# Two PSUM banks in turn for the products with v and three instead of four for scores and maxima, from the MLP's third chunk on

## The chip, the cores and the metric

The kernel runs on one core of one Trainium2 chip. Its time is device microseconds of one execution: the median of 3 runs of the kernel before is 1242.78 us (1240.4 to 1245.14). The core's engines work in parallel, each through its own instructions in order: PE (TensorE, with its weight loads shown apart as PEld), DVE (VectorE), ACT (ScalarE), POOL (GpSimd) and SP, which here issues DMAs. They wait for each other through semaphores.

Matmul results go to PSUM, which this kernel uses as eight banks, 0 to 7, each a tile of 128 x 512 fp32 numbers that holds one matmul's result or one running sum at a time. Before PE may write a bank anew, the engine that reads the old content must be done with it.

## The reference

64 heads (8 batches of 8), 576 positions, head size 64; then an MLP over 4608 tokens, 512 to 2048 to 512. All in fp32.

```python
log_f = np.log(np.clip(f, 0.0001, 1.0))
cum = np.cumsum(log_f, axis=-1)
scores = (q @ k.T) / sqrt(64) + cum[:, None] - cum[None, :]
scores = where(causal, -1e9, scores)
scores = scores - max(scores)                 # over a row
attn = exp(scores); attn = attn / (sum(attn) + 1e-9)
x = attn @ v                                  # heads side by side: 4608 x 512
h = maximum(x @ w_in, 0)
out = (h * h) @ w_out
```

## The kernel before, in words

**Attention.** A head is cut into six units (`UNITS`), each a piece of the transposed scores: one block of up to 128 keys against a stretch of 64 to 448 queries. The loop at its end goes through *slots*, one unit of one head each, six slots to a head. In a slot:

- the unit's **score** (L352 and L355 for the heads from the fifteenth on, L346 before): one bank of the turn `s`. ScalarE reads it with Exp into `p` (L365), GpSimd masks the diagonal (L367), and at the next slot's start the result is split in two parts for fp32 accuracy: `ph` by ScalarE (L380), `pl` by VectorE (L381).
- the **product with v** of the unit two slots back (L390, L391, L392: the parts pl and ph against the parts of v). The late queries of a head (256 to 575) are summed over five units in one bank of the turn `av`; the early ones (0 to 255) are done in the head's last such slot in another tile of that turn. When a sum is complete, ScalarE copies it out, the values by L426 and the denominators by L427. A head's first product (unit 0, late queries, 128x320) comes one slot after the early queries of the head before.
- of the head after it, the row **maxima**, six to a head in slots 1 to 4, here called m0 to m5 (L313: 256, 320, 448, 320, 192 and 64 columns). VectorE masks and reduces each in its bank (L319, two instructions: the reduction and the reading of its accumulator). Once the MLP runs, the maxima have no banks of their own; they draw from the turn `s`, as the scores do (`m=[]`, so that `bank` takes `banks["s"]`).

**MLP.** The tokens go in 18 chunks of 256, and a chunk in 16 steps. A step has two halves: `mlp1` (L478, 12 matmuls of 256 columns into the bank `h`; then Relu r and its square gh by ScalarE, L486 and L488; r times r, g, and its remainder gl by VectorE, L487 and L489) and, for the step before, `mlp2` (L501, 6 matmuls of 512 columns into the banks `o0` and `o1`, which hold a chunk's output through its 16 steps). `fill` spreads these halves over the slots, so that PE has them between the attention's short matmuls. When a new chunk's x is due, VectorE splits it (L465, L466).

**Order.** The order on PE, ScalarE, VectorE and GpSimd is the order in which the program is written (`in_order`). So an instruction that waits holds up everything behind it on its engine.

**Banks.** `bank(use)` takes the first number of a use's list and puts it at the end. The uses' lists change as the program goes on: with the first chunk of the MLP, the second and the third (`mlp_half`). The third chunk begins while the eighteenth head is under way, and its lists stay to the end. From then on: bank 4 for h, 6 and 7 for the outputs, and 0, 1, 2, 3, 5 for attention.

Of the kernel before, what the change touches and what calls it, by code (L numbers as in the profile page):

```python
# [33 lines left out]
def decay_attention_relu2_kernel(  # L34
# [45 lines left out]
    banks = {"av": [0, 6], "s": [1, 2, 3], "m": [4, 5], "h": [4], "o0": [6], "o1": [7]}  # L80
# [373 lines left out]
    def split_x(c, finished):  # L454

        if c >= NCHUNK:
            return
        if ("x", c) not in mst:
            mst["x", c] = [wk.tile([P, NCC, T], F32R, name=x, bufs=1) for x in xnames[c % 2]], c * T
        (xh, xl), t0 = mst["x", c]  # L460
        while t0 < (c + 1) * T and t0 // S < finished:
            b = t0 // S
            t1 = min((b + 1) * S, (c + 1) * T)
            o, i = slice(t0 - c * T, t1 - c * T), slice(t0 - b * S, t1 - b * S)
            nc.vector.tensor_copy(out=xh[:, :, o], in_=xts[b][:, :, i])  # L465
            nc.vector.tensor_tensor(  # L466
                out=xl[:, :, o], in0=xts[b][:, :, i], in1=xh[:, :, o].bitcast(F32), op=ALU.subtract,
            )
            t0 = t1
        mst["x", c] = (xh, xl), t0  # L470

    def mlp1(c, fc):
        xh, xl = mst["x", c][0]
        ph = bank("h")
        w = split_w[2 * fc].rearrange("p s (c f) -> p s c f", f=P)
        for k, (s, x) in enumerate(((1, xh), (0, xh), (0, xl))):
            for cc in range(NCC):
                nc.tensor.matmul(  # L478
                    ph[:, :T], w[:, s, cc], x[:, cc, :],
                    start=(cc == 0 and k == 0), stop=(cc == NCC - 1 and k == 2),  # L480
                )
        r = wk.tile([P, T], F32, name="r", bufs=1)
        g = wk.tile([P, T], F32, name="g", bufs=1)
        gh = wk.tile([P, T], F32R, name="gh")
        gl = wk.tile([P, T], F32R, name="gl")
        nc.scalar.activation(out=r, in_=ph[:, :T], func=AF.Relu)  # L486
        nc.vector.tensor_tensor(out=g, in0=r, in1=r, op=ALU.mult)  # L487
        nc.scalar.activation(out=gh, in_=r, func=AF.Square)  # L488
        nc.vector.tensor_tensor(out=gl, in0=g, in1=gh.bitcast(F32), op=ALU.subtract)  # L489
        mst["g", c, fc] = (gh, gl)  # L490

    def mlp2(c, fc):
        if fc == 0:
            mst["o", c] = [bank(f"o{t}") for t in range(NTT)]
        gh, gl = mst.pop(("g", c, fc))
        w = split_w[2 * fc + 1]
        for t in range(NTT):
            po = mst["o", c][t]
            ts = slice(t * P, (t + 1) * P)
            for k, (g, s) in enumerate(((gh, 1), (gl, 0), (gh, 0))):  # L500
                nc.tensor.matmul(  # L501
                    po, g[:, ts], w[:, s],
                    start=(fc == 0 and k == 0), stop=(fc == NF - 1 and k == 2),
                )
            if fc == NF - 1:
                osb = wk.tile([P, DM], F32, name="osb")
                nc.scalar.copy(out=osb, in_=po)
                nc.sync.dma_start(out=out[c * T + t * P:c * T + (t + 1) * P, :], in_=osb)
# [5 lines left out]
    def next_step():  # L514

        for c in range(NCHUNK):
            fc = ahead[c]
            if fc < NF and len(split_w) >= 2 * (fc + 1):
                return c, fc
            if fc < NF and c > 0:  # L520
                return None

    def mlp_half(finished):
        if halves[0] % 2:
            if len(steps) > 1:
                mlp2(*steps[-2])
        else:
            step = next_step()
            if step is None:
                return False  # L530
            c, fc = step
            if fc == 0:
                if c == 0:
                    banks.update(s=[1, 2, 3, 5], m=[], av=[0])
                if c == 1:
                    banks.update(s=[1, 2], o0=[3], o1=[5])
                if c == 2:
                    banks.update(s=[1, 2, 3, 5], o0=[6], o1=[7])
                split_x(c, finished)
            if fc > 0 and ("x", c + 1) not in mst and (c != 1 or ahead[0] == NF):  # L540
                split_x(c + 1, finished)
            mlp1(c, fc)
            ahead[c] += 1
            steps.append(step)
        halves[0] += 1
        return True
# [35 lines left out]
    def fill(n, part):  # L582

        b = sum(r <= n for r in ready)
        if b == 0:
            return
        r0 = ready[b - 1]
        r1 = ready[b] if b < B else r0 + H * NU
        limit, before = (2 * NF * (x * S // T) for x in (b, b - 1))
        goal = before + (limit - before) * (n - r0 + part) / (r1 - r0)  # L590
        if b == 1 and len(split_w) == NW:

            if not pace:
                pace.append((n + part, halves[0]))
            n0, h0 = pace[0]
            goal = h0 + (limit - h0) * (n + part - n0) / (r1 - n0)
        while halves[0] < min(goal, limit):
            split_last()
            if not mlp_half(b):
                break  # L600
# [71 lines left out]
    while halves[0] < 2 * NCHUNK * NF:  # L672
        mlp_half(B)
# [41 lines left out]
```

## Time and profile before

| | |
|---|---|
| median of 3 runs | 1242.78 us |
| the profiled execution | 1241.21 us |
| its span, first to last instruction | 1239.5 us |
| PE busy | 1179.0 us, 95% |
| PEld (weight loads, beside PE) | 1047.0 us, 84% |
| VectorE busy | 785.6 us, 63% |
| ScalarE busy | 701.3 us, 57% |
| GpSimd busy | 383.4 us, 31% |
| granted TensorE clock, mean | 0.992 |

PE is the engine with the least room. It is busy 95% of the span, and after the first fifth nearly all of the time; the attention of the first heads, with the weights' preparation beside it, fills that first fifth. From about 1090 us on only the MLP is left.

The trace gives each instruction's start and duration. For matmuls the end is modelled, so that consecutive ones overlap on paper: a matmul of 320 columns is shown as some 0.31 us long while the next starts 0.15 us after it. PE can thus wait without an idle gap being shown, and the distance from one start to the next tells more than the gaps.

### The profile page before, as it was taken

To read this page: it belongs to the slowest core of one execution; us is meant where nothing else is said; L and a number is where in the kernel's file an instruction comes from. 1 tells how busy PE (TensorE), PEld (TensorE's weight loads), DVE (VectorE), ACT (ScalarE), POOL (GpSimd) and SP (SyncE) were. 2 spreads that over 40 slices of the span, in tenths; PEclk is the share of its full clock that TensorE was granted. 3 is DMA by queue.
4 is the path that set the end of the run, shared out by engine and by line. 5 is a ranking of instruction groups with operands and counts; after the bars stand their busy time and mean duration, and the time that the engine had idled before them with its cause. 6 is when DMAs were issued, how large, how long until landed. Compare 5 with 4: busy or idle time off the path is not lost.

```text
span 1239.5 us, 23297 instructions
## 1 busy us (share of the span) xinstructions
PE 1179.0 (95%) x7652; PEld 1047.0 (84%) x7652; DVE 785.6 (63%) x2042; ACT 701.3 (57%) x1720; POOL 383.4 (31%) x576
## 2 busy tenths in 40 slices
PE   3777899999999999999999999999999999999998
PEld 2555677888999899999899989998999899999997
DVE  7658777667676767666656666677676767533332
ACT  3555455566666666665565666666666666632332
POOL 4333223333333433333222233334333333200000
PEclk9998899999999999999999999999999999999999
DMA  8867631112121212121202121211121212000000
GB/s 198 181 145 182 165 100 27 51 33 58 41 58 33 51 32 58 41 58 26 58 17 53 32 58 36 54 36 49 41 58 41 58 41 58 12 27 1 18 18 17
DMA packets 115640, 71.91 MB, mean 58 GB/s; under 512 B 97384, under 2 KB 97384, under 8 KB 115520
## 3 DMA queue, kind: packets, MB, share of 16 engines
q1 hardware_dynamic: 114400, 66.30, 21.9%
q0 software_dynamic: 1120, 4.13, 1.6%
q8 instruction: 61, 1.00, 0.3%
q14 instruction: 59, 0.48, 0.1%
HBM read 60.20 MB, written 9.88 MB: 57 GB/s over the span
## 4 chain that ended last, share of the span: by engine, by line
PE 62%; ACT 2%; issue 2%; POOL 1%; DMA 0%; DVE 0%; SPq 0%; POOLq 0%; DVEq 0%; ACTq 0%
PE bank L478 25%; PE bank L501 24%; PE bank L390 3%; PE bank L313 2%; PE bank L355 2%; PE bank L392 2%; PE bank L391 2%; PE bank L352 2%; DMA den<-rdr 0%; ACT r L486 0%; ACT den L427 0%; ACT p L365 0%; ACT ph L380 0%; ACT rl L281 0%; POOL xt L448 0%
## 5 line engine op out<-in xcount | busy, mean ns | idle before, releaser
L501 PE MATMUL bank<-w,gh 128*128 128x512 f32 x1152 | 413.1, 399 | 0.0
L478 PE MATMUL bank<-xh,w 128*128 128x256 f32 x2304 | 329.8, 286 | 4.5 <-DVE tcol L319 4.4
L381 DVE TENSOR_TENSOR pl<-p,ph 128x320 fp32r<-128x320 f32 (+4 forms) x300 | 187.0, 623 | 199.7 <-ACT ph L380 191.0
L478 PEld LDWEIGHTS bank<-xh,w 128*128 128x128 f32 x2304 | 301.4, 190 | 12.2 <-DVE tcol L319 4.7
L501 PEld LDWEIGHTS bank<-w,gh 128*128 128x128 f32 x1152 | 217.0, 188 | 38.5
L486 ACT ACTIVATE r<-bank 128x256 f32<-128x256 f32 x288 | 110.4, 383 | 207.5 <-PE bank L478 194.3
L501 PE MATMUL bank<-w,gl 128*128 128x512 f32 x576 | 226.7, 394 | 0.2 <-DVE gl L489 0.2
L487 DVE TENSOR_TENSOR g<-r 128x256 f32<-128x256 f32 x288 | 126.4, 439 | 140.7 <-ACT r L486 139.9
L367 POOL TENSOR_SCALAR_AFFINE_SELECT p<-p 128x128 f32<-128x128 f32 (+1 forms) x250 | 82.4, 329 | 429.4 <-ACT p L365 269.0
L380 ACT CAST ph<-p 128x320 fp32r<-128x320 f32 (+4 forms) x300 | 124.4, 415 | 149.5 <-POOL p L367 147.7
L478 PE MATMUL bank<-xl,w 128*128 128x256 f32 x1152 | 184.9, 283 | 0.0
L319 DVE CUSTOM_DVE_ANT_0 bank<-bank,mz 128x256 f32<-128x256 f32 (+4 forms) x320 | 133.6, 432 | 42.2 <-PE bank L313 34.6
L478 PEld LDWEIGHTS bank<-xl,w 128*128 128x128 f32 x1152 | 158.4, 191 | 0.0
L489 DVE TENSOR_TENSOR gl<-g,gh 128x256 fp32r<-128x256 f32 x288 | 129.7, 450 | 35.7 <-ACT p L365 0.9
L365 ACT ACTIVATE p<-bank 128x320 f32<-128x320 f32 (+4 forms) x300 | 115.8, 386 | 63.9 <-PE bank L355 52.3
L313 PE MATMUL bank<-rk 66*128 66x320 f32 (+9 forms) x384 | 112.5, 319 | 26.9 <-DMA rk<-qkraw 14.8
L488 ACT ACTIVATE gh<-r 128x256 fp32r<-128x256 f32 x288 | 120.5, 418 | 9.2
L501 PEld LDWEIGHTS bank<-w,gl 128*128 128x128 f32 x576 | 109.1, 189 | 14.2 <-DVE gl L489 0.9
L313 PEld LDWEIGHTS bank<-rk 66*128 66x128 f32 (+3 forms) x384 | 68.8, 185 | 43.0 <-DVE tcol L319 18.2
L390 PE MATMUL bank<-pl,vh 128*65 128x320 f32 (+4 forms) x350 | 96.9, 277 | 2.3 <-ACT den L427 2.3
L391 PE MATMUL bank<-ph,v 128*64 128x320 f32 (+4 forms) x350 | 94.8, 271 | 0.0
L392 PE MATMUL bank<-ph,vh 128*65 128x320 f32 (+4 forms) x350 | 93.1, 272 | 0.0
(73 smaller groups left out, 1514.4 us busy)
## 6 DMA issues: line engine op xcount, KB each, us to landing
qkraw<-in_qk SPq DMA_DIRECT2D x50, 288.0 KB
v<-in_v SPq DMA_DIRECT2D x64, 160.0 KB
den<-rdr SPq DMA_DIRECT2D x64, 144.0 KB
out<-osb SPq DMA_DIRECT2D x36, 256.0 KB
w<-in_w_in SPq DMA_DIRECT2D x16, 512.0 KB
w<-in_w_out SPq DMA_DIRECT2D x16, 512.0 KB
rl<-in_qk SPq DMA_DIRECT2D x14, 288.0 KB
rk<-in_qk POOLq DMA_DIRECT2D x14, 288.0 KB, 5.0
```

The costliest lines, as they stand in the source:

```text
L313: nc.tensor.matmul(ps[:m, :n], st["r2"][:rows, q0:q0 + m], st["kl0"][:rows, k0:k0 + n], start=True, stop=True,)
L319: nc.vector.tensor_tensor_reduce(out=ps[:m, :n], in0=ps[:m, :n], in1=mz[:m, mo:mo + n], op0=ALU.add, op1=ALU.min, scale=-1.0, scalar=init, ...
L380: nc.scalar.copy(out=ph[:, :n], in_=p[:, :n])
L381: nc.vector.tensor_tensor(out=pl[:, :n], in0=p[:, :n], in1=ph[:, :n].bitcast(F32), op=ALU.subtract,)
L390: nc.tensor.matmul(acc[:D + 1, o], vh, pl[:, i], start=first, stop=False)
L391: nc.tensor.matmul(acc[:D, o], vl, ph[:, i], start=False, stop=False)
L392: nc.tensor.matmul(acc[:D + 1, o], vh, ph[:, i], start=False, stop=last)
L478: nc.tensor.matmul(ph[:, :T], w[:, s, cc], x[:, cc, :], start=(cc == 0 and k == 0), stop=(cc == NCC - 1 and k == 2),)
L487: nc.vector.tensor_tensor(out=g, in0=r, in1=r, op=ALU.mult)
L488: nc.scalar.activation(out=gh, in_=r, func=AF.Square)
L489: nc.vector.tensor_tensor(out=gl, in0=g, in1=gh.bitcast(F32), op=ALU.subtract)
L501: nc.tensor.matmul(po, g[:, ts], w[:, s], start=(fc == 0 and k == 0), stop=(fc == NF - 1 and k == 2),)
```

## The change

One line, in the lists that hold from the third chunk on. The products with v get a second bank, 5, in turn with 0, and the turn that scores and maxima share loses it.

```diff
                 if c == 2:
-                    banks.update(s=[1, 2, 3, 5], o0=[6], o1=[7])
+                    banks.update(s=[1, 2, 3], av=[0, 5], o0=[6], o1=[7])
```

No instruction is added, removed or moved: PE, VectorE, ScalarE, GpSimd and SP have the same instructions in the same order. What differs is whom an instruction waits for. On PE, in the third slot of a head, after the score of its unit 2 (the numbers behind `bank_` count tiles, not banks; `x8` stands for eight alike; DVE is VectorE):

```order
-L390 MATMUL bank_3457<-pl,vh_81 65x320 [waits DVE_49,PE_49,Activation_49]
-L391 MATMUL bank_3457<-ph,v 64x320 [waits Pool_49]
+L390 MATMUL bank_3457<-pl,vh_81 65x320 [waits DVE_49,PE_49]
+L391 MATMUL bank_3457<-ph,v 64x320 [waits Activation_49,Pool_49]
 L392 MATMUL bank_3457<-ph,vh_81 65x320
-L313 MATMUL bank_3461<-rk_76 128x320
+L313 MATMUL bank_3461<-rk_76 128x320 [waits Activation_49]
 L478 MATMUL bank_3469<-xh_2103,w_1055 128x256 x8
 L478 MATMUL bank_3469<-xl_2104,w_1055 128x256 x4
-L313 MATMUL bank_3492<-rk_76 128x448
+L313 MATMUL bank_3492<-rk_76 128x448 [waits DVE_49]
```

The head's first product with v (L390) no longer waits for ScalarE; L391 does, for the part ph. The maximum of 448 columns (m2) now waits for VectorE, whose reduction of m0 is the last reader of its bank. In the next slot, m3 and m4 on PE:

```order
 L390 MATMUL bank_3457<-pl,vh_81 65x320
-L391 MATMUL bank_3457<-ph,v 64x320 [waits Activation_49]
+L391 MATMUL bank_3457<-ph,v 64x320
 L392 MATMUL bank_3457<-ph,vh_81 65x320
-L313 MATMUL bank_3512<-rk_76 128x320 [waits Activation_49]
+L313 MATMUL bank_3512<-rk_76 128x320 [waits DVE_49]
 L313 MATMUL bank_3517<-rk_76 128x192 [waits DVE_49]
```

m4 (192 columns) waits for VectorE in both; its bank's last reader was the reduction of m1 before, and is that of m2 now.

## Rows read from the trace of the kernel before

**Rows 1.** Stretch 278 to 1090 us: PE, PEld, DVE, ACT, POOL busy, PEclk, DMA

```profile
278.00:1090.00 812.00, 808.70 (x5506) 737.48 (x5505) 541.03 (x1455) 510.89 (x1272) 284.63 (x439) 1.00 0.18 44
```

**Rows 2.** Timeline near 310 us: start, duration, engine, line, what it does

```profile
308.58 0.49 DVE L381 TENSOR_TENSOR pl<-p,ph 128x320 fp32r<-128x320 f32 x1
...
309.99 0.37 ACT L427 COPY den<-bank 1x256 f32<-1x256 f32 x1
...
310.21 0.27 PE L355 MATMUL bank<-rl 128*128 128x192 f32 x1
310.41 0.36 PE L390 MATMUL bank<-pl,vh 128*65 128x320 f32 x1
310.61 0.30 PE L391 MATMUL bank<-ph,v 128*64 128x320 f32 x1
```

**Rows 3.** Timeline of PE at the same place near 691 us

```profile
691.41 0.28 PE L355 MATMUL bank<-rl 128*128 128x192 f32 x1
691.53 0.31 PE L390 MATMUL bank<-pl,vh 128*65 128x320 f32 x1
691.68 0.30 PE L391 MATMUL bank<-ph,v 128*64 128x320 f32 x1
```

**Rows 4.** Timeline of PE at the same place near 294 us

```profile
293.53 0.27 PE L355 MATMUL bank<-rl 128*128 128x192 f32 x1
...
294.37 0.31 PE L391 MATMUL bank<-ph,v 128*64 128x320 f32 x1
```

**Rows 5.** Timeline 312 to 315 us, VectorE up to m2's end, PE's m4

```profile
312.91 0.36 DVE L381 TENSOR_TENSOR pl<-p,ph 128x192 fp32r<-128x192 f32 x1
313.18 0.42 DVE L487 TENSOR_TENSOR g<-r 128x256 f32<-128x256 f32 x1
...
314.59 0.14 DVE L319 DVE_READ_ACCUMULATOR2_ANT tcol<- 128x1 f32 x1
...
314.76 0.25 PE L313 MATMUL bank<-rk 66*128 66x192 f32 x1
```

**Rows 6.** The same near 330 us; x2 is m3 and m4

```profile
328.98 0.35 DVE L381 TENSOR_TENSOR pl<-p,ph 128x192 fp32r<-128x192 f32 x1
329.32 0.43 DVE L487 TENSOR_TENSOR g<-r 128x256 f32<-128x256 f32 x1
...
330.74 0.14 DVE L319 DVE_READ_ACCUMULATOR2_ANT tcol<- 128x1 f32 x1
...
330.83 0.40 PE L313 MATMUL bank<-rk 66*128 66x320 f32 x2
```

**Rows 7.** The same near 298 us

```profile
298.28 0.14 DVE L319 DVE_READ_ACCUMULATOR2_ANT tcol<- 128x1 f32 x1
...
298.40 0.40 PE L313 MATMUL bank<-rk 66*128 66x320 f32 x2
```

**Rows 8.** Timeline of PE near 278 us, before the third chunk's lists

```profile
277.69 0.41 PE L313 MATMUL bank<-rk 66*128 66x320 f32 x1 [1.75 <-DVE tcol L319]
277.94 1.11 PE L478 MATMUL bank<-xh,w 128*128 128x256 f32 x8
```

**Rows 9.** Timeline near 413 us: PE's m4, VectorE's end of m2

```profile
412.68 0.25 PE L313 MATMUL bank<-rk 66*128 66x192 f32 x1
...
413.40 0.14 DVE L319 DVE_READ_ACCUMULATOR2_ANT tcol<- 128x1 f32 x1
```

**Rows 10.** Timeline near 541 us: PE's m2, VectorE's end of m0

```profile
541.17 0.36 PE L313 MATMUL bank<-rk 66*128 66x448 f32 x1
...
541.67 0.13 DVE L319 DVE_READ_ACCUMULATOR2_ANT tcol<- 128x1 f32 x1
```

**Rows 11.** Timeline near 607 us: PE's mlp2 after m2, VectorE's end of m0

```profile
606.47 0.39 PE L501 MATMUL bank<-w,gh 128*128 128x512 f32 x1
607.04 0.50 PE L501 MATMUL bank<-w,gl 128*128 128x512 f32 x1 [0.18 <-DVE gl L489]
...
607.25 0.14 DVE L319 DVE_READ_ACCUMULATOR2_ANT tcol<- 128x1 f32 x1
```

## The prediction

> **What bounds the kernel now.** [...] Next I read PE's own order of time around one thing only, the first product with v of a head (L390 at 128x320), because the edit gives it another bank. At 310.41 it starts 0.05 us after ScalarE's copy of the preceding accumulator's denominators ends (309.99 + 0.37 = 310.36), in the bank that this copy reads [rows 2]. That it waits does not show as idle time, since the end of the matmul before is modelled; it shows in the distance of starts. From L355 to L391 it is 0.40 us here and 0.27 us at 691.41, where L390 did not wait [rows 2, 3]. The head has lost 0.13 us. At 293.53 the same distance is 0.84 us, a loss of 0.57 [rows 4].
>
> Going through the stretch head by head, 35 of the 47 heads have L390 starting within 0.06 us of that copy's end: 16 like the first, 12 in between, 7 like the last. The other heads lie mostly between 550 and 720 us, where two steps of the MLP fall on each slot and the copy is long done. Counting the in-between ones like the first, the waits are worth 28 x 0.13 + 7 x 0.57 = 7.6 us. This is the most that the edit can save.
>
> **What the change removes.** With two banks in turn, a head's early-query half takes bank 0 and its late-query half bank 5. L390 then waits for a copy that ended half a head ago, so all 7.6 us of waiting at this place go. What is late next there is VectorE's pl for the same unit, and that ends at 308.58 + 0.49 = 309.07, 1.3 us before L390 [rows 2]. No instruction is added or moved on any engine; the DMA queues keep their order too.
>
> **What it adds: a wait of the maxima.** Scores and maxima share one turn, which is now three banks long. A head has six maxima, m0 to m5 (L313, columns 256, 320, 448, 320, 192, 64), among six scores s0 to s5, in PE's order s1, m0, s2, m1, m2, s3, m3, m4, s4, m5. With four banks m2 took the bank of s1 and m4 that of m1; with three, m2 takes that of m0, and m4 that of m2. ScalarE's exponentials are early everywhere, so the scores' places change nothing. But VectorE is late with m0 and m2. Behind a waiting matmul stands all of PE's later work, for its order is fixed.
>
> At an ordinary head of the first kind VectorE is done with m2 at 314.59 + 0.14 = 314.73, and PE starts m4 at 314.76 [rows 5]. A wait released by VectorE would let it start some 0.06 us after that, at 314.79. That is 0.03 us later than it starts now, *although* PE was late by the wait at L390. Now the question is whether VectorE gets earlier when PE does. It doesn't: its chain (pl, m0, m1, pl, g, gl, m2) starts from ScalarE's rounding of p, which stands behind the copies and not behind L390; and between the second pl (312.91) and g (313.18) there are 0.27 us, as close as these two ever come [rows 5]. So here the saving is lost whole, and PE ends up 0.03 us behind where it was.
>
> In the second kind (330.83 for the pair m3, m4; so m4 at about 330.98) VectorE ends m2 at 330.74 + 0.14 = 330.88, so m4 could start at 330.94, 0.04 us earlier than now; and g follows pl after 0.34 instead of 0.27, since it waited for ScalarE's r, that is for PE, so VectorE itself can be 0.07 earlier [rows 6]. Together 0.10 to 0.11 us may be kept. In the seven heads with the long wait, m4 is at about 298.55 and VectorE's m2 ends at 298.42 [rows 7]: 0.07 + 0.07 = 0.14 us may be kept out of 0.57.
>
> **The price of a wait itself.** When PE waited for VectorE at 277.69, the next matmul started 0.25 us after the waiting one; a 128x320 matmul that waits for nothing takes 0.15 from start to start [rows 3, 8]. So each hit costs 0.10 us more, the weight load that no longer hides under the matmul before. Nothing in this stretch shows a loss on L313 at a bank wait of this ring, so I bound the restart: from below nothing, from above twice 0.10 in a head where m2 and m4 both wait. I take once 0.10, since m4 comes last and the time lost at m2 is then time that m4 need not wait.
>
> [...]
>
> **Heads in which VectorE is held up.** In five heads VectorE splits the MLP's next x (L465, L466) just then, and m0 and m2 come much later. Near 412 us it ends m2 at 413.40 + 0.14 = 413.54, so m4 can start at 413.60, against 412.68 now: 0.92 + 0.10 = 1.02 us [rows 9]. Three heads are like this (410, 846, 977 us): 3.06. Near 541 us m2 itself waits: VectorE ends m0 at 541.67 + 0.13, so 541.86 against 541.17, 0.69 + 0.10 = 0.79 [rows 10]. Near 606 us VectorE ends m0 at 607.25 + 0.14 = 607.39, so m2 can start at 607.45; now it starts at about 606.26 (the 0.21 us of its 448 columns, by proportion from 320, ahead of L501 at 606.47): 1.19 + 0.10 = 1.29. From it goes a wait for gl that then is covered: L501 at 606.47 is followed at 607.04, 0.57 where 512 columns need about 0.24, and its restart of 0.10: 0.43 saved, 0.86 left [rows 11].
>
> **The sum**, against the profiled execution:
> - 14 heads of the first kind: 14 x (0.03 + 0.10) = +1.82
> - 12 of the second: 12 x (0.10 - 0.10) = 0
> - 7 with the long wait: 7 x (0.10 - 0.14) = -0.28
> - the five with the split of x: 3.06 + 0.79 + 0.86 = +4.71
> - the other heads, all before 278 and after 1090 us: 0
>
> Together +6.2 us. (The first kind has 16 heads at L390; one of them is the first of the stretch, and one is in the five.) The profiled execution took 1241.21 us, 1.57 below the median of the runs shown; so 1247.4 by its own time, and 1249.0 beside the median of 1242.78. Half a per cent, about what a measurement of this kernel can tell from no change, is 6.2 us: the forecast stands on that line.
>
> **Rivals.**
> 1. *The copies go and little comes back: not slower.* Were VectorE's chain released by PE in the ordinary heads, it would move up with PE, m4 would find its bank free, and only the five heads would wait. Then -7.6 + 4.7 = -2.9: 1239.9. It decides wherever g waits for r rather than for pl. For it: the second kind shows such a wait, of 0.07. Against: the first kind shows none, and the room at m4 there is below zero already. [...]
> 2. *The restart is free:* 14 x 0.03 - 12 x 0.10 - 7 x 0.14 + 3 x 0.92 + 0.69 + 0.76 = +2.4 or so: 1245.2. For it: 0.10 rests on waits of the stretch before. Against: L390 shows the same kind of loss after its waits, 0.20 to its successor instead of 0.15 [rows 2, 3].
> 3. *Later maxima make VectorE late for something else*, pl or gl, and PE pays a second time: another 0.10 us in each of 47 heads, 4.7 more, 10.9 in all: 1253.7. For it: VectorE runs on without a pause from pl to g and gl [rows 5]. Against: its pl for a head's first unit is 1.3 us early [rows 2].
> 4. *The change does not take the wait away*: excluded by the waits of the two programs, where ScalarE no longer stands at L390.
>
> **How the numbers follow.** Forecast 0.60 (1246 to 1252, for 0.05 to 0.15 a restart and the same for the seven heads); rival 1 0.12, rival 2 0.14, rival 3 0.14. Slower by over 0.5% is half of the forecast and rival 3, 0.44; faster is the far end of rival 1, 0.03; the rest, 0.53, is within. The range leaves out rival 1 and half of rival 3: 1243.5 to 1254.
>
> **What would show it right or wrong.** L390's waits for ScalarE are gone from the list of waits, and L355 to L391 is 0.27 in every head. In its place L313 waits for VectorE (tcol L319): about 38 places, the longest near a microsecond at the five splits, and most of the others a pair of starts at m4 that has grown without idle time. VectorE's busy time stays within a few us of 785.6. The forecast is wrong if L313 has no waits outside the five heads (rival 1), if its successor starts 0.15 after it (rival 2), or if L390 or L501 wait for VectorE instead (rival 3).

## The result and the profile after

| | before | after |
|---|---|---|
| median of 20 runs each, side by side | 1241.52 us | 1247.38 us |
| ratio, 95% interval | | 1.0037 (1.0025 to 1.0048) |
| the profiled execution | 1241.21 us | 1249.67 us |
| PE busy | 1179.0 us | 1183.9 us |
| VectorE busy | 785.6 us | 784.9 us |

The changed kernel is slower by 0.25 to 0.48%, 3.1 to 6.0 us; the forecast was 6.2 us. Of the 8.46 us between the two profiled executions 3.5 us lie ahead of the third chunk, where both kernels have the same lists, and say nothing of the change. So from here on a kernel is compared from the start of the third chunk's first matmul (L478, at 277.94 us before and 281.46 after) to the start of the last L501 (1235.48 and 1243.89): 957.54 us before, 962.43 after, 4.89 us more.

First the list of what PE waited for, from 283 to 1100 us of the changed kernel (engine, line, waited-for engine and line: us in total, times, longest):

```profile
PE bank L313 <- DVE tcol L319: 3.3, 5, 1.0
PE bank L313 <- DVE rk L280: 0.7, 2, 0.5
```

The same list for the kernel before, 279 to 1100 us, begins:

```profile
PE bank L390 <- ACT den L427: 2.3, 7, 0.4
...
PE bank L501 <- DVE gl L489: 0.2, 1, 0.2
```

The waits of L390 for ScalarE's copies are gone, as is the one for gl; L313 waits for VectorE's reductions instead. The five waits listed are only those that leave an idle gap on paper. By the distance of starts there are many more: counting maxima that start 0.03 to 0.08 us after the end of the reduction that last reads their bank, the changed kernel has 26 at m2 (all heads of the first kind, of the long wait and of the split) and 36 at m4 (all of the first three kinds and three with the split), in 46 heads; by the same count the kernel before has none. PE's activity over the same stretch as [rows 1], in the changed kernel:

```profile
278.00:1090.00 812.00, 806.01 (x5461) 731.54 (x5461) 540.96 (x1455) 508.78 (x1269) 286.24 (x443) 1.00 0.18 44
```

There are 5461 matmuls against 5506 in the same 812 us: the kernel is 3.5 us late when the stretch begins, and loses the rest on the way. The granted clock is 1.00 in both, and PE still looks busy throughout: 806 us. The loss hides in the distances. Next the timeline of PE at the place of [rows 2], 3.5 us later (start, duration, engine, line, what it does):

```profile
313.69 0.27 PE L355 MATMUL bank<-rl 128*128 128x192 f32 x1
313.80 0.30 PE L390 MATMUL bank<-pl,vh 128*65 128x320 f32 x1
313.94 0.31 PE L391 MATMUL bank<-ph,v 128*64 128x320 f32 x1
...
318.25 0.36 PE L313 MATMUL bank<-rk 66*128 66x192 f32 x1
318.45 0.31 PE L478 MATMUL bank<-xh,w 128*128 128x256 f32 x1
```

L355 to L391 is 0.25 us where it was 0.40: the wait that the edit is about is gone. m4 (192 columns) follows 4.5 us later, and the next matmul starts 0.20 after it. In the kernel before, that next matmul stands at

```profile
314.85 1.13 PE L478 MATMUL bank<-xh,w 128*128 128x256 f32 x8
```

which is 0.09 after the m4 of [rows 5]. What m4 waited for is in VectorE's timeline of the same head, which answers to [rows 5]:

```profile
316.38 0.35 DVE L381 TENSOR_TENSOR pl<-p,ph 128x192 fp32r<-128x192 f32 x1
316.65 0.42 DVE L487 TENSOR_TENSOR g<-r 128x256 f32<-128x256 f32 x1
317.17 0.43 DVE L489 TENSOR_TENSOR gl<-g,gh 128x256 fp32r<-128x256 f32 x1
317.51 0.63 DVE L319 CUSTOM_DVE_ANT_0 bank<-bank,mz 128x448 f32<-128x448 f32 x1
318.06 0.14 DVE L319 DVE_READ_ACCUMULATOR2_ANT tcol<- 128x1 f32 x1
```

From pl to g are 0.27 us, as before, so VectorE had no idle time there to give up. It ends m2 at 318.20, and m4 starts 0.05 after that. Behind L390 PE was 0.14 us ahead of its old pace. It gives 0.11 of that back at m2, which here waits too (for m0), and the rest at m4; the restart behind m4 costs 0.11 more, and the head ends 0.13 behind.

PE's step from one head's m4 to the next one's, after minus before, by the kinds of the prediction, in us over the whole stretch:

| | 14 first kind | 12 second kind | 7 long wait | 5 split of x | the rest | whole |
|---|---|---|---|---|---|---|
| predicted | +1.82 | 0 | -0.28 | +4.71 | 0 | +6.2 |
| changed kernel | +1.68 | -0.25 | -0.86 | +4.47 | -0.14 | +4.9 |
| changed kernel, later run | +1.61 | -0.22 | -0.83 | +5.30 | -0.15 | +5.7 |

The heads between 550 and 720 us, but for the split near 606, move by 0.00 each.

### The profile page after: what moved, and what is told of

Same layout as the page of the kernel before. It is cut to its first block, busy times and chain, and to the rows that moved or that the text cites. A ratio compares the mean times of both kernels' runs of the same rounds, so it can differ in the third digit from the quotient of the medians.

```text
span 1248.0 us, 23354 instructions
## 1 busy us (share of the span) xinstructions
PE 1183.9 (95%) x7652; PEld 1047.8 (84%) x7652; DVE 784.9 (63%) x2042; ACT 700.7 (56%) x1720; POOL 382.6 (31%) x576
## 5 line engine op out<-in xcount | busy, mean ns | idle before, releaser
L501 PE MATMUL bank<-w,gh 128*128 128x512 f32 x1152 | 413.3, 399 | 0.0
L478 PE MATMUL bank<-xh,w 128*128 128x256 f32 x2304 | 329.7, 286 | 5.3 <-DVE tcol L319 5.3
L381 DVE TENSOR_TENSOR pl<-p,ph 128x320 fp32r<-128x320 f32 (+4 forms) x300 | 190.2, 634 | 200.6 <-ACT ph L380 189.9
L478 PEld LDWEIGHTS bank<-xh,w 128*128 128x128 f32 x2304 | 301.5, 190 | 12.9 <-DVE tcol L319 5.7
L501 PEld LDWEIGHTS bank<-w,gh 128*128 128x128 f32 x1152 | 217.0, 188 | 38.7
L501 PE MATMUL bank<-w,gl 128*128 128x512 f32 x576 | 226.6, 393 | 0.0
L367 POOL TENSOR_SCALAR_AFFINE_SELECT p<-p 128x128 f32<-128x128 f32 (+1 forms) x250 | 81.3, 325 | 437.3 <-ACT p L365 308.4
L478 PE MATMUL bank<-xl,w 128*128 128x256 f32 x1152 | 184.8, 283 | 0.0
L478 PEld LDWEIGHTS bank<-xl,w 128*128 128x128 f32 x1152 | 158.5, 191 | 0.0
L313 PE MATMUL bank<-rk 66*128 66x320 f32 (+9 forms) x384 | 120.8, 338 | 29.0 <-DVE tcol L319 13.4
L501 PEld LDWEIGHTS bank<-w,gl 128*128 128x128 f32 x576 | 109.1, 189 | 13.8 <-DVE gl L489 0.4
L313 PEld LDWEIGHTS bank<-rk 66*128 66x128 f32 (+3 forms) x384 | 70.3, 185 | 53.1 <-DVE tcol L319 24.4
L390 PE MATMUL bank<-pl,vh 128*65 128x320 f32 (+4 forms) x350 | 95.0, 272 | 0.0
L391 PE MATMUL bank<-ph,v 128*64 128x320 f32 (+4 forms) x350 | 94.9, 271 | 0.0
```

Of the source, the lines that this page charges most:

```text
L313: nc.tensor.matmul(ps[:m, :n], st["r2"][:rows, q0:q0 + m], st["kl0"][:rows, k0:k0 + n], start=True, stop=True,)
L381: nc.vector.tensor_tensor(out=pl[:, :n], in0=p[:, :n], in1=ph[:, :n].bitcast(F32), op=ALU.subtract,)
L390: nc.tensor.matmul(acc[:D + 1, o], vh, pl[:, i], start=first, stop=False)
L478: nc.tensor.matmul(ph[:, :T], w[:, s, cc], x[:, cc, :], start=(cc == 0 and k == 0), stop=(cc == NCC - 1 and k == 2),)
L501: nc.tensor.matmul(po, g[:, ts], w[:, s], start=(fc == 0 and k == 0), stop=(fc == NF - 1 and k == 2),)
```

## The experiments

My theory: a head's VectorE chain does not come earlier when PE does, so the copies' waits are worth nothing while the same head ends in a wait for m2's reduction; and three banks for scores and maxima cost a restart per head and the five splits. Rivals: the two halves of the edit add up (saving and price independent of each other); or the price lies elsewhere than at m4 and m2.

**The changed kernel once more**, in the same session as the next three:

> The changed kernel once more on this chip, as the measure for the others: 4 to 6 us above before, ratio 1.0037 within 0.001.

Measured: 1.0046 (1.0029 to 1.0063). In its trace the ordinary heads repeat to a few hundredths; the split near 977 us costs 2.31 instead of 1.57, since x and the keys behind it came later there (more on this below).

**Only the loss of the bank**: the products with v keep one bank, and bank 5 stays idle.

```diff
-                    banks.update(s=[1, 2, 3, 5], o0=[6], o1=[7])
+                    banks.update(s=[1, 2, 3], o0=[6], o1=[7])
```

> The loss alone: the turn of scores and maxima has three banks, the products with v keep their one bank, and bank 5 lies idle. Theory (PE is held at m4 by VectorE's end of m2 whatever happened at L390 before, so the saving at L390 is swallowed): about 7 us above before (+0.6%), hardly more than the changed kernel, since L390's waits for ScalarE, worth 7.6 us, lie in front of waits that end at a fixed time anyway. By head: 14 heads of the first kind +0.13 each, as in the changed kernel; the 12 of the second some +0.05 instead of 0; the 7 with the long wait near 0 instead of a gain of 0.18. Rival (the two halves of the change simply add): the loss of the changed kernel, 4.9 us, plus the whole saving given back, 7.6 us: +12.5 us, or 1.0%.

Measured: 1.0048 (1.0031 to 1.0066), and by its trace +6.4 us from the third chunk on. The list of waits from 279 to 1100 us:

```profile
PE bank L313 <- DVE tcol L319: 3.3, 5, 1.0
PE bank L390 <- ACT den L427: 1.9, 6, 0.4
...
```

Both waits stand here side by side, and the kernel is about as slow as with the first of them alone. So taking away the wait at L390, 7.6 us in the kernel before, is worth 0.7 to 1.5 us by the traces (6.4 less 5.7 or 4.9) once m2 and m4 wait, and by the medians nothing that shows: the halves don't add up. In the 33 ordinary heads (the first three kinds), which repeat better than the splits, it is 1.5 us: +2.06 here, +0.57 in both traces of the changed kernel. PE that is held at L390 merely arrives later at a bank that would not have been free earlier. By the distance of starts m2 waits at 6 places there and m4 at 17, against 26 and 36.

**Only the gain**: bank 0 for the late queries, and the early half of a head draws its bank from the shared turn, which keeps all four.

```diff
-            st["av"] = bank("av")
+            st["av"] = bank("lo" if low and "lo" in banks else "av")
...
-                    banks.update(s=[1, 2, 3, 5], o0=[6], o1=[7])
+                    banks.update(s=[1, 2, 3, 5], lo=[], o0=[6], o1=[7])
```

> The saving without the loss: scores and maxima keep four banks, and only the late queries' sum keeps bank 0; the early queries' sum, which is begun and ended in one slot, takes the next bank of the turn of four. L390 then has a bank that was copied out a slot ago, and m2 and m4 stand four places behind their bank's last user. Theory: no wait at L390, none at L313 in the ordinary heads; 7.6 us less than before, and another 1.2 us where a wait of mlp1 for ScalarE behind it goes too: 8 to 9 us below before, -0.7%. Rival (VectorE's chain or ScalarE's copies hold PE next, at pl, gl or the bank h): less than half of that, under 4 us, with new waits of L390 or L501 in the list.

Measured: 0.9943 (0.9925 to 0.9962), by the trace -7.7 us: 0.09 to 0.21 in each head of the first two kinds, mostly 0.15, and 0.53 on average in one with the long wait. Of the further 1.2 us that I expected behind it nothing shows. Its PE, and VectorE's end of m2, in the head shown above:

```profile
312.02 0.27 PE L355 MATMUL bank<-rl 128*128 128x192 f32 x1
312.13 0.30 PE L390 MATMUL bank<-pl,vh 128*65 128x320 f32 x1
312.27 0.31 PE L391 MATMUL bank<-ph,v 128*64 128x320 f32 x1
...
316.27 0.40 PE L313 MATMUL bank<-rk 66*128 66x320 f32 x2
316.50 1.13 PE L478 MATMUL bank<-xh,w 128*128 128x256 f32 x8
...
316.54 0.14 DVE L319 DVE_READ_ACCUMULATOR2_ANT tcol<- 128x1 f32 x1
```

L390 doesn't wait, and m3 and m4 together take 0.23 us before L478, though VectorE ends m2 only at 316.68: m4 has m1's bank again. The 7.6 us were there to be had. What takes them back is the missing bank of the maxima.

**The changed kernel with m4 half a slot later**, and m5 after it:

```diff
-        for i, x in enumerate(MAXIMA[split]):
+        for i, x in enumerate(MAXIMA[split] if h < 19 else (1.5, 2, 2.5, 3, 4, 4.5)):
```

> The changed kernel with the maxima m4 and m5 half a slot later (from the twentieth head on), so that an MLP half or the score s4 stands between m2 and m4, and m4's bank is one that ScalarE left. Theory: the ordinary heads' waits at m4 go, those of m2 in the heads with the split of x stay. By the changed kernel's trace the starts after m2 stand 0.05 us earlier than before in the first kind, 0.17 in the second, 0.3 in the third, and 4 us later in all in the five with the split: -0.6 - 2.0 - 2.0 + 4.0 = about -0.6 us against before, 5 us below the changed kernel. Rival (the loss at m4 is VectorE's backlog and moves to the next instruction that needs it): as the changed kernel, 4 to 6 us above before.

Measured: 1.0001 (0.9988 to 1.0014), by the trace +1.1 us. The same place:

```profile
317.45 0.27 PE L313 MATMUL bank<-rk 66*128 66x192 f32 x1
...
315.19 0.14 DVE L319 DVE_READ_ACCUMULATOR2_ANT tcol<- 128x1 f32 x1
```

m4 now comes 2.1 us after m2's reduction (315.33), and no m4 of the trace waits. The 26 waits at m2 stay, those of the splits among them, and with them PE comes out where it began: 1.1 us above before instead of the 0.6 below that I expected. The miss lies mostly in the seven heads with the long wait, where m2 waits too: they gained some 0.1 us in all instead of 2.0. So 3.8 us (4.9 - 1.1) of the price lie at m4; the next version shows where the rest is.

**The changed kernel with m2 later as well**, half a slot, and all behind it:

```diff
-        for i, x in enumerate(MAXIMA[split]):
+        for i, x in enumerate(MAXIMA[split] if h < 19 else (1.5, 2, 3, 3.5, 4, 4.5)):
```

> The changed kernel with its maxima spread further (from the twentieth head on m2 half a slot later, beside m3, and m4 and m5 half a slot later too), so that m2's bank is one that ScalarE left and a slot lies between m2 and m4. Theory (the whole loss is the two waits of the three-bank turn for VectorE's m0 and m2): none of them is left, the heads with the split of x included, and L390's saving of 7.6 us stays: 6 to 8 us below before, like the kernel with the early queries in the turn of four (-7.1 measured). Rival (the five heads lose because VectorE is late for PE's other work, not for a bank): some 4 us of loss stay, 2 to 4 us below before.

Measured, in a second session: 0.9933 (0.9913 to 0.9953), by the trace -6.2 us. The waits of 283 to 1100 us that are left:

```profile
PE bank L313 <- DVE rk L280: 0.9, 2, 0.7
PE bank L501 <- DVE gl L489: 0.4, 1, 0.4
PE bank L313 <- DVE tcol L319: 0.3, 1, 0.3
```

By the distance of starts no m2 or m4 waits for a reduction any more; the one wait for tcol is an m5's. So three banks do, if the maxima stand further apart; moving m2 gave 7.3 us beyond moving m4: 3.2 each in the five splits and the seven heads with the long wait, 1.5 in the first kind, and 0.6 lost elsewhere. The kernel before was not run with its maxima moved alike, so what the move is worth with four banks is not shown. This kernel and the one with the shared early half both beat the kernel before, by about 0.6%; their intervals overlap.

**VectorE delayed on purpose.** Two small additions to a 9-column tile that nobody reads stand on VectorE ahead of m2's reduction, once in the changed kernel and once in the kernel before. If PE's pace is set by m2's reduction in the one and not in the other, the first pays for them and the second doesn't.

```diff
+    pad = cpool.tile([P, 9], F32, name="pad")
+    nc.gpsimd.memset(pad, 0.0)
...
+            if h > 18 and i == 3:
+                for _ in range(2):
+                    nc.vector.tensor_scalar_add(pad, pad, 1.0)
```

> The changed kernel with two small additions on VectorE (128x9, on a tile that nothing else uses) just before the reduction m2 of each head from the twentieth on, some 0.4 us by the rows of the additions at L439 (0.17 long, the next 0.20 after it). Theory (PE stands at m4 until VectorE has ended m2): PE pays the 0.4 us in all of the 33 ordinary heads and in the 3 with the split where m4 waits, and not between 550 and 720 us: 36 x 0.4 = +14 us on the changed kernel, 19 us above before (1.5%). Rival (VectorE has room, and the loss is the weight load alone): within 2 us of the changed kernel.

> The same additions in the kernel before, with four banks. Theory: m4's bank is that of m1, which VectorE has left 0.7 us or more before, so the 0.4 us are hidden: within 1 us of before, ratio 1.000 within 0.0015. Rival (VectorE's lateness reaches PE by another way too, such as pl or gl): 5 us or more above before.

Measured: 1.0111 (1.0084 to 1.0137) with three banks, 0.9997 (0.9982 to 1.0013) with four. VectorE in the first of them (the line numbers are up to 5 higher in this version, so the reduction is L324):

```profile
317.50 0.43 DVE L494 TENSOR_TENSOR gl<-g,gh 128x256 fp32r<-128x256 f32 x1
317.84 0.38 DVE L323 TENSOR_SCALAR pad<-pad 128x9 f32<-128x9 f32 x2
318.12 0.62 DVE L324 CUSTOM_DVE_ANT_0 bank<-bank,mz 128x448 f32<-128x448 f32 x1
```

From gl to m2's reduction are 0.62 us instead of 0.34 in the rows of the changed kernel: a delay of 0.28, not the 0.4 behind my expectation. PE pays for it about one for one in the heads of the first two kinds, 0.20 to 0.42 us a head and 7.9 in all, and little in the heads between 550 and 720 us, 0.3 in all: 8.5 us over the changed kernel by the traces, where I expected 14. Besides the smaller delay, the seven heads with the long wait fall short: the first adds 0.32, the six later ones -0.02 to 0.20 each. PE does wait at their m4, but VectorE comes through the split of x ahead of them without the delay that PE paid in the head before, and PE gets that back there (near 867 us of the changed kernel's time the delay has made PE 5.96 us later, VectorE 5.77). With four banks it pays nothing (-0.1 us): there VectorE's reductions were hidden.

## Why the prediction was right, point by point

**The wait that goes** went whole: 7.6 us read from the distances of starts (some 7.9 when each head is taken by itself: the twelve in between lose 0.18, not 0.13, and two of the seven 0.47, not 0.57); the version that only takes it away gains 7.7 by the trace and 0.38 to 0.75% (4.7 to 9.3 us), by the interval of its runs.

**VectorE does not follow PE** [rows 5]. In the heads of the first kind the forecast was 0.03 + 0.10 each, 1.82; 1.68 came, 0.06 to 0.21 a head. The delay that is paid one for one with three banks and not at all with four shows that m2's reduction sets the pace there. Some 38 waits were forecast and 62 came, most of the further ones at m2; but the time lost at m2 is time that m4 need not wait, as the prediction had it, so that a head of the first kind, in which both wait, loses 0.12 on average and not 0.10 more. In the second kind g follows pl after 0.27 now, where it was 0.34 in [rows 6]; PE's m2 in that head of the changed kernel, and then VectorE:

```profile
332.14 0.37 PE L313 MATMUL bank<-rk 66*128 66x448 f32 x1
332.34 0.40 PE L501 MATMUL bank<-w,gh 128*128 128x512 f32 x1
...
332.59 0.35 DVE L381 TENSOR_TENSOR pl<-p,ph 128x192 fp32r<-128x192 f32 x1
332.86 0.42 DVE L487 TENSOR_TENSOR g<-r 128x256 f32<-128x256 f32 x1
```

The 0.07 us by which VectorE can be earlier were read rightly, and the term of 0 became -0.02 a head.

**The restart** cost what was said, [rows 8]: L478 after m4 comes 0.20 us after it instead of 0.09, and L501 after a waiting m2 0.31 (414.47 to 414.78 below) instead of 0.20 (332.14 to 332.34, where m2 did not wait). That is 0.11 for 0.10; neither trace shows a free restart behind such a wait, and rival 2 falls. The weight load that is no longer hidden is the waiting matmul's own (see the last section).

**The five splits**: 4.47 for 4.71, but singly they are off, and the sum came out so near partly by luck. VectorE's work in these heads follows x, which GpSimd makes (L448) when a DMA has brought the denominators (den<-rdr); the prediction took that time to be as far from PE's as before. The kernel before near the first of the five, GpSimd's x and PE's m0:

```profile
404.44 1.43 POOL L448 TENSOR_TENSOR xt<-xt,den 128x576 f32<-128x576 f32 x1 [2.12 <-DMA den<-rdr]
407.84 0.39 PE L313 MATMUL bank<-rk 66*128 66x256 f32 x1 [0.35 <-DVE rk L280]
```

The changed kernel at the same place, then VectorE and PE near the second, the third and the last:

```profile
407.75 1.43 POOL L448 TENSOR_TENSOR xt<-xt,den 128x576 f32<-128x576 f32 x1 [1.88 <-DVE gl L489]
411.15 0.39 PE L313 MATMUL bank<-rk 66*128 66x256 f32 x1
414.47 0.47 PE L313 MATMUL bank<-rk 66*128 66x448 f32 x1 [0.61 <-DVE tcol L319]
414.78 0.40 PE L501 MATMUL bank<-w,gh 128*128 128x512 f32 x1
...
545.70 0.13 DVE L319 DVE_READ_ACCUMULATOR2_ANT tcol<- 128x1 f32 x1
...
612.57 0.40 PE L501 MATMUL bank<-w,gh 128*128 128x512 f32 x1
612.81 0.39 PE L501 MATMUL bank<-w,gl 128*128 128x512 f32 x1
...
979.90 0.43 DVE L465 CAST xh<-xt 128x512 fp32r<-128x512 f32 x1 [2.07 <-POOL xt L448]
981.84 0.39 PE L313 MATMUL bank<-rk 66*128 66x256 f32 x1 [0.46 <-DVE rk L280]
```

The first came to 0.58 instead of 1.02. PE had come to this head 3.76 us later than before (3.52 and 0.24 lost on the way), x only 3.31 (404.44 to 407.75), and so the keys that VectorE splits behind x (rk, L280). PE's m0, which waited for these keys in the kernel before, is only 3.31 later too (407.84 to 411.15): PE has won 0.45 us there. From there on it loses 1.03, where 1.02 was forecast. The last is the other way round: x comes 7.39 later where PE has come 6.83 later, so PE loses 0.56 at m0 and then 1.01 at m2 and m4: 1.57 in all. The fourth is 0.94: 1.03 from m0 on, less 0.09 that PE won ahead of that. In the second, 0.55 for 0.79, VectorE's m0 ends 4.03 later (545.70 to 541.67 in [rows 10]) where PE had come 4.28 later; from VectorE's time PE loses 0.80. The third is 0.83 for 0.86; at 612.81 the wait for gl is gone (0.24 after its predecessor, where [rows 11] has 0.57). So the price of a split was right in each, and when x comes differs from run to run: the last head costs 2.31 in the later run of the same kernel, where PE stands 1.17 us idle at m0, and 0.25 in the version that only takes the wait away. Why x comes sooner or later is not shown. (In the changed kernel's row of the first x the wait is put down to gl, which ended just before; x has several waits, and the list names the last.)

**The mis-sized term** is that of the seven heads with the long wait: -0.86 for -0.28, the largest part (0.58 of 1.3 us) of what lies between 6.2 and 4.9; the second kind and the splits have a quarter of a microsecond each. The step that failed is that the room at m4 there, 0.14 us [rows 7], was reckoned as if VectorE kept its distance to PE up to that head. It doesn't. First the kernel before, GpSimd, VectorE, ScalarE and PE ahead of the head near 495 us (in brackets: idle time of the engine just before, and what ended it):

```profile
480.85 0.96 DVE L466 TENSOR_TENSOR xl<-xt,xh 128x768 fp32r<-128x768 f32 x1
481.42 0.55 POOL L367 TENSOR_SCALAR_AFFINE_SELECT p<-p 128x128 f32<-128x128 f32 x1 [1.15 <-DVE xh L465]
485.00 0.41 ACT L380 CAST ph<-p 128x256 fp32r<-128x256 f32 x1 [2.15 <-POOL p L367]
487.37 0.31 PE L352 MATMUL bank<-rk 67*128 67x320 f32 x1
```

And the same four in the changed kernel:

```profile
485.05 0.96 DVE L466 TENSOR_TENSOR xl<-xt,xh 128x768 fp32r<-128x768 f32 x1
485.77 0.39 POOL L367 TENSOR_SCALAR_AFFINE_SELECT p<-p 128x128 f32<-128x128 f32 x1 [1.31 <-DVE xh L465]
489.20 0.41 ACT L380 CAST ph<-p 128x256 fp32r<-128x256 f32 x1 [2.06 <-POOL p L367]
491.70 0.31 PE L352 MATMUL bank<-rk 67*128 67x320 f32 x1
```

VectorE's split is 4.20 us later than before, PE 4.33: the 0.13 are left of what PE lost at m4 of the head ahead, and VectorE, by which it was held, has not lost them. GpSimd's mask starts with PE's results (4.35 later) but ends 0.15 us after the split in both, 481.97 and 486.16, so with VectorE; its next mask, ScalarE's ph (4.20 later) and the head's reductions follow. So m4's bank comes free 0.13 us earlier against PE: -0.04 - 0.13 = -0.17, and the six later heads measure -0.08 to -0.20. At the first of the seven it goes the other way: PE had gained 0.18 in the head ahead of it, and the head measures +0.13, where -0.04 + 0.18 is 0.14. That is read from the traces; no run moved the split by itself, but in the changed kernel with VectorE delayed PE gets back there, too, what it had paid ahead.

**The rivals.** 1 (little comes back) falls by the 62 waits and by the sum. 3 (VectorE late for pl or gl) falls: no such wait is in the list after, L355 to L391 is 0.25 or 0.26 in 43 of 46 heads and in the other three, all with the split, 0.35 to 0.40 (0.35 before), and the delayed VectorE cost PE 8.5 us, less than its 0.28 in each of the 36 heads that wait at m4. 4 falls by the list of waits.

## What to carry to other kernels

A wait is worth only what is left of it at the next wait behind it whose end does not move (here 0.7 to 1.5 of 7.6 us): before pricing its removal, ask what releases that one, and whether the releasing engine would come earlier too. What a bank of a ring was worth here went by its slowest reader, VectorE's reduction (with the two additions ahead of it PE lost 8.5 us with three banks and nothing with four). A sum that lives briefly could draw from the common ring, and maxima set further apart needed a bank less: each gave 0.6% with the same eight banks with which the changed kernel lost 0.4%.

## What the runs showed of the hardware

- A mask on GpSimd (L367, 128x128) that starts under VectorE's split of x (L466, xl<-xt,xh) ends 0.15 us after the split: in 16 of 17 cases in the two traces, with durations from 0.39 to 1.17 us. What holds the mask there is not shown. Here it ties GpSimd, ScalarE and PE to VectorE's order of time: in the rows near 481 and 485 us ScalarE's ph is 4.20 us later, as the split is, where the mask starts 4.35 later.
- A matmul that waited for its bank cost 0.11 us beside the wait at m4 (0.20 to the next start for 0.09) and at m2 (0.31 for 0.20), and no idle time shows it. After a waiting L390 it is 0.05 (0.20 in [rows 2] for 0.15 in [rows 3]). It is the load of the waiting matmul's own weights, which elsewhere begins under the matmul before. The weight loads (PEld) at m3, which nothing holds up (its matmul starts at 318.05, 0.14 behind its load), and at the m4 of the changed kernel shown above:

```profile
317.91 0.19 PEld L313 LDWEIGHTS bank<-rk 66*128 66x128 f32 x1
318.25 0.19 PEld L313 LDWEIGHTS bank<-rk 66*128 66x128 f32 x1 [0.16 <-DVE tcol L319]
318.36 0.30 PEld L478 LDWEIGHTS bank<-xh,w 128*128 128x128 f32 x2
```

m4's load waits with it, and the next load starts 0.11 later. The price went by the columns of the waiting matmul's weights, not of its successor's: 0.11 us for 128 at m2 and m4, 0.05 for 65 at L390, whose successor has 64. The wait of an m5 in the version with m2 moved tells the two apart, since m5 has 64 and its successor 128:

```profile
544.96 0.24 PE L313 MATMUL bank<-rk 66*64 66x64 f32 x1 [0.32 <-DVE tcol L319]
545.03 0.47 PE L501 MATMUL bank<-w,gh 128*128 128x512 f32 x1
```

From start to start are 0.08 us before rounding, where an m5 that doesn't wait has 0.03: 0.05 more, as at L390.
